# Theta from float16 parts of x that DMA turns, v kept from its sizing, and a new order of the steps: a planned attention and mixing kernel on one core

## The chip, the cores and the metric

The kernel runs on one core of one Trainium2 chip. The metric is the device time of one execution in microseconds; several runs are made and their median is taken. The engines are TensorE (PE; its weight loads are shown apart as PEld), VectorE (DVE), ScalarE (ACT), GpSimd (POOL) and SyncE (SP), which issues the DMA transfers.

## The reference

```python
def _attn_ref(q, k, v):                      # 8 batches, 8 heads, 576 rows, 64 columns
    scores = scale * np.matmul(q, k.transpose(0, 1, 3, 2))
    scores = np.where(block_i >= block_j, scores, -1000000000.0)   # blocks of 64 rows
    attn = np.exp(scores - np.max(scores, axis=-1, keepdims=True))
    attn = attn / (np.sum(attn, axis=-1, keepdims=True) + 1e-09)
    return np.matmul(attn, v)

def _moe_ref(x, w_theta, w_tok_r, w_tok_i, w_ch):   # x: 8 x 576 x 512, the heads side by side
    theta = x @ w_theta
    zr, zi = x * np.cos(theta), x * np.sin(theta)
    u = x + np.einsum('ts,bsd->btd', w_tok_r, zr) + np.einsum('ts,bsd->btd', w_tok_i, zi)
    return u + np.maximum(u @ w_ch, 0.0)
```

q, k, v are float32, the weights float64 (read as two words each). Theta is large, so its product has to be accurate.

## The kernel before, in words

Every product is made in parts: an operand is rounded to a short type (the high part) and what is left is rounded again (the low part); high x high, low x high and high x low are added in PSUM. q, k, theta's x, u, w_theta and w_ch have float32r parts, p (the exponentials), v, z and w_tok float16 parts.

Two heads are a pair, four pairs a batch. Per pair q and k are loaded, rounded on GpSimd (L471, L475), and their low parts made on VectorE for q (L479) and on GpSimd for k (L484). TensorE makes the scores (L506, L520, the mask L514), VectorE the row maxima (L533), ScalarE the exponentials (L537) and their high part (L546), VectorE their low part (L549). A DMA transposition (L553, `pt<-p`, 24 or 26 blocks of 128x128 for one head) turns them, and TensorE multiplies them by v (L565, L570); VectorE divides by the row sums into `xn` (L577, L579, L585).

v is scaled by a power of two per batch so that its float16 parts hold. For that all four pairs' v are loaded into `vz` (L436), ScalarE sums their sizes (L439), GpSimd spreads the sums on a diagonal (L324), TensorE brings them together (L328) and VectorE makes the power (L335 to L344). Later each v is loaded once more, into `v` (L488), for its parts (L491, L494). x comes out scaled in the same way.

Per batch the mixer follows. TensorE transposes x, 20 blocks (L623); ScalarE rounds it out of PSUM and removes the scale (`xh`, L634), VectorE makes the low part (`xl`, L638). Theta (L647) is 5 groups of 12 matmuls of 512 columns. Its turns and remainders come from L655 and L660, sizes, cosines and sines from ScalarE (L666 to L674), the products with x from GpSimd (L682), their parts z from L691 and L696. The mixing over tokens (L706) is 8 groups of 27 matmuls of 288 columns; VectorE adds the high part of x to it (L711), GpSimd the low part (L716). u's parts are made by ScalarE (L719) and GpSimd (L723), the channel product (L731) is 8 groups of 12 matmuls, VectorE finishes (L737) and the result is stored (L741).

The weights are prepared while batch 0 runs. Each float64 row block is loaded as words (L370). ScalarE scales the high word, read as a float32, by 2^-112 (L379), VectorE shifts it (L386), puts the sign back (L388) and adds the low word's bits (L391). w_tok is sized as v is, over all its blocks (L395, L413 to L423), and its parts are made on ScalarE (L399) and VectorE (L405); those of w_theta and w_ch on ScalarE (L401) and GpSimd (L408).

What runs when is a list. Every step is added under a key with the steps that it needs; `TIMES` holds one number per step, the steps are issued in the order of these numbers, each engine takes its own in that order, and `BANKS` names the PSUM bank that each step takes. The numbers only sort:

```python
    order = sorted(zip(TIMES, range(len(TIMES)), parts), key=lambda x: x[:2])
```

A tile used again needs the steps that read it last (`turn_of`).

Of the kernel before, what the change touches and what calls it, by code (L numbers as in the profile page):

```python
# [27 lines left out]
QK_BUFS = 2  # L28
# [5 lines left out]
    845, 1285, 1406, 1509, 1716, 1838, 1919, 315, 755, 830, 880, 1012, 1094, 1175, 1150, 2754, 3004, 3252, 3631,  # L34
    3713, 4155, 1430, 2267, 3150, 3318, 3563, 3645, 3869, 1825, 2610, 3699, 3803, 3995, 4128, 9220, 9303, 2105,
    2550, 3114, 3186, 3735, 3817, 9286, 9383, 3875, 4394, 4521, 4629, 4960, 5042, 9020, 9223, 3695, 4334, 4557,
    5405, 5539, 5670, 8781, 9703, 4235, 4675, 5276, 5339, 5471, 5821, 8715, 9017, 4055, 4495, 4593, 5607, 6229,
    6311, 9484, 9623, 5095, 5610, 7069, 7181, 7315, 7403, 9418, 9543, 6245, 6710, 6903, 6995, 7113, 7269, 8847,
    8937, 5615, 6055, 6297, 6400, 7247, 7336, 9352, 9463, 7205, 7645, 7863, 8223, 8375, 8457, 8538, 7510, 7950,
    8113, 8289, 8690, 8913, 9097, 7790, 8230, 11402, 11530, 11734, 11981, 12305, 8635, 9696, 9783, 9932, 10224,  # L40
    10548, 10767, 7627, 7809, 8111, 8355, 8535, 8607, 8633, 8682, 0, 345, 495, 840, 1025, 1370, 1610, 1986, 2085,
    2113, 2164, 2205, 2239, 2261, 2283, 2475, 2285, 2670, 3570, 3915, 4415, 4760, 5400, 5888, 6015, 6057, 6268,
    6476, 6939, 6987, 7061, 7105, 6425, 6770, 7080, 7470, 8510, 9116, 9245, 9612, 9819, 9887, 9938, 10130, 10216,
    10292, 10489, 11331, 9945, 10325, 10424, 10854, 11089, 11517, 11859, 12231, 12495, 12519, 12650, 12738, 12865,
    12927, 13096, 13118, 12444, 13954, 14053, 14434, 14533, 14878, 15088, 15486, 15596, 15730, 18326, 18393, 18427,
# [900 lines left out]
```

## Time and profile before

| | |
|---|---|
| median of 3 runs | 780.52 us (779.15 to 782.35) |
| the profiled execution | 782.25 us, its span 780.3 us |
| mean granted TensorE clock | 0.969 |
| share of the span: PE, PEld, DVE, ACT, POOL | 89%, 75%, 71%, 64%, 52% |
| read from HBM, written | 54.59 MB, 9.44 MB |
| moved by DMA | 117.66 MB, of 232420 packets 209680 under 512 B |

Busy PE time counts matmuls that overlap, with ends that are modelled; so lengths of long runs of matmuls in the chain of waits are the better price of TensorE's work. A group in the table of groups is one line, engine, operation and shape; its last column is the idle time of the engine just before and what ended it.

### The profile page before, as it was taken

How to read it: one execution, taken by the hardware profiler on the slowest of the kernel's cores; microseconds unless marked ns; L12 is line 12 of the kernel's file. 1: busy time of each engine (PE TensorE's matmuls, PEld its weight loads, DVE VectorE, ACT ScalarE, POOL GpSimd, SP SyncE). 2: the span in 40 equal slices, each digit the busy share in tenths (PEclk: the TensorE clock that was granted, in tenths of full speed). 3: DMA queues.
4: the chain of work that ended last, by engine and by line, in shares of the span. 5: the costliest groups of instructions: out<-in, count | busy, mean ns of one | idle time of the engine just before them, and what ended most of it. 6: DMA issues, size and time to landing. Idle time of an engine off the chain costs nothing.

```text
span 780.3 us, 18483 instructions
## 1 busy us (share of the span) xinstructions
PE 695.9 (89%) x7657; PEld 588.8 (75%) x7657; DVE 551.4 (71%) x995; ACT 499.4 (64%) x780; POOL 408.5 (52%) x413
## 2 busy tenths in 40 slices
PE   3536479788999999999999999999999999999987
PEld 2435368676897878887898788878898889778866
DVE  5799998669757895688955987397847985543221
ACT  4778788866885776756793577466774678335220
POOL 3331332883348660886348552974178613850860
PEclk9986779999999999999999999999999999999999
DMA  8989997688838995469735785596736962430101
GB/s 286 226 266 273 235 216 202 163 167 206 198 95 205 200 198 120 95 134 193 166 132 105 156 157 136 117 176 146 155 102 120 201 140 65 78 76 1 61 1 61
DMA packets 232420, 117.66 MB, mean 151 GB/s; under 512 B 209680, under 2 KB 209680, under 8 KB 232336
## 3 DMA queue, kind: packets, MB, share of 16 engines
q1 hardware_dynamic: 232336, 116.48, 64.4%
q8 instruction: 60, 0.98, 0.5%
q14 instruction: 24, 0.20, 0.1%
HBM read 54.59 MB, written 9.44 MB: 82 GB/s over the span
## 4 chain that ended last, share of the span: by engine, by line
PE 61%; DMA 12%; DVE 12%; POOL 5%; issue 5%; ACT 4%; POOLq 0%; ACTq 0%; SPq 0%; DVEq 0%
PE ps L706 18%; PE ps L647 14%; PE ps L731 13%; DMA pt<-p 10%; PE ps L506 7%; PE ps L565 6%; DVE m L533 3%; DVE p L549 2%; DMA vz<-in_v 2%; DVE v L494 1%; POOL u L716 1%; ACT t L537 1%; ACT p L546 1%; POOL ul L723 1%; POOL zl L696 1%
## 5 line engine op out<-in xcount | busy, mean ns | idle before, releaser
L537 ACT ACTIVATE t<-ps,m 128x576 f32<-128x576 f32 (+4 forms) x288 | 143.5, 553 | 74.0 <-DVE m L533 55.8
L706 PE MATMUL ps<-wT_h,zh 128*128 128x288 f16 x576 | 166.7, 289 | 5.3 <-ACT t L537 4.3
L706 PE MATMUL ps<-wT_h,zl 128*128 128x288 f16 x576 | 166.2, 289 | 2.4 <-POOL zl L696 1.8
L706 PE MATMUL ps<-wT_l,zh 128*128 128x288 f16 x576 | 166.3, 289 | 0.0
L533 DVE TENSOR_REDUCE m<-ps 128x1 f32<-128x192 f32 (+4 forms) x288 | 133.6, 510 | 19.2 <-PE ps L514 17.3
L549 DVE SCALAR_TENSOR_TENSOR p<-t,p 128x1536 f16<-128x1536 f32 (+1 forms) x64 | 124.3, 1944 | 31.9 <-ACT p L546 31.8
L706 PEld LDWEIGHTS <-zh 128*128 128x128 f16 x1152 | 113.5, 99 | 31.1 <-ACT zh L691 1.1
L565 PE MATMUL ps<-v,pt 128*128 128x65 f16 x2688 | 98.5, 198 | 30.1 <-DVE xn L585 22.3
L565 PEld LDWEIGHTS <-pt 128*128 128x128 f16 x2688 | 93.5, 101 | 36.1 <-DMA pt<-p 18.2
L546 ACT ACTIVATE p<-t 128x1536 f16<-128x1536 f32 (+1 forms) x64 | 96.6, 1516 | 36.3 <-DMA pt<-p 35.9
L682 POOL TENSOR_TENSOR aa<-aa,xn 128x256 f32<-128x256 f32 (+1 forms) x96 | 70.2, 758 | 75.6 <-PE ps L731 27.9
L506 PE MATMUL ps<-kh,qh 64*128 64x64 f32 (+4 forms) x384 | 73.0, 360 | 20.2 <-ACT t L537 10.9
L731 PE MATMUL ps<-uh,wch_h 128*128 128x288 f32 x256 | 78.3, 306 | 1.8 <-ACT uh L719 1.6
L731 PE MATMUL ps<-ul,wch_h 128*128 128x288 f32 x256 | 76.3, 298 | 1.1 <-POOL ul L723 1.1
L731 PE MATMUL ps<-uh,wch_l 128*128 128x288 f32 x256 | 76.3, 298 | 0.0
L706 PEld LDWEIGHTS <-zl 128*128 128x128 f16 x576 | 56.9, 99 | 22.1 <-POOL zl L696 5.2
L723 POOL TENSOR_TENSOR ul<-u,uh 128x576 fp32r<-128x576 f32 x32 | 56.4, 1769 | 23.8 <-ACT uh L719 23.8
L716 POOL TENSOR_TENSOR u<-u,xl 128x576 f32<-128x576 f32 x32 | 47.5, 1490 | 39.6 <-DVE u L711 30.3
L737 DVE SCALAR_TENSOR_TENSOR u<-ps,u 128x288 f32<-128x288 f32 x64 | 29.1, 455 | 55.3 <-PE ps L731 54.2
L506 PEld LDWEIGHTS ps<-kh,qh 64*128 64x128 f32 x384 | 41.6, 201 | 33.1 <-ACT t L537 13.2
L647 PE MATMUL ps<-wth_h,xh 128*128 128x512 f32 x160 | 65.3, 408 | 1.3 <-DVE xl L638 1.3
L506 PE MATMUL ps<-kh,ql 64*128 64x64 f32 (+4 forms) x384 | 64.9, 327 | 0.0
(98 smaller groups left out, 1490.9 us busy)
## 6 DMA issues: line engine op xcount, KB each, us to landing
vz<-in_v SPq DMA_DIRECT2D x32, 384.0 KB, 3.9
v<-in_v SPq DMA_DIRECT2D x32, 384.0 KB, 3.8
q<-in_qT SPq DMA_DIRECT2D x32, 320.0 KB, 3.5
k<-in_kT SPq DMA_DIRECT2D x32, 288.0 KB, 3.7
out<-u SPq DMA_DIRECT2D x32, 288.0 KB, 2.1
w_raw<-in_w_tok SPq DMA_DIRECT2D x9, 576.0 KB, 4.4
w_raw<-in_w_theta SPq DMA_DIRECT2D x4, 512.0 KB, 6.2
w_raw<-in_w_ch SPq DMA_DIRECT2D x4, 512.0 KB, 5.0
```

Of the source, the lines that this page charges most:

```text
L506: nc.tensor.matmul(s[hh][:, col:col + n], lhsT=qq[rows, i * P:(i + 1) * P], rhs=kk[rows, k0:k0 + n], start=nn == 0 and col % BANK == 0, st ...
L533: nc.vector.tensor_reduce(out=m, in_=s, axis=AX.X, op=ALU.max, negate=True)
L537: nc.scalar.activation(out=to, in_=s, func=AF.Exp, scale=1.0, bias=m)
L546: nc.scalar.mul(self.p[:, 0, 0:self.width], self.t, LIFT)
L549: nc.vector.scalar_tensor_tensor(out=self.p[:, 1, 0:self.width], in0=self.t, scalar=LIFT, in1=self.p[:, 0, 0:self.width], op0=ALU.mult, op ...
L565: nc.tensor.matmul(o[:, i, :], lhsT=pp[:, block, :], rhs=vv[:, of, hh, :], start=nn == 0, stop=nn == n - 1)
L647: nc.tensor.matmul(g, lhsT=xx[:, dt, i * P:(i + 1) * P], rhs=ww[:, dt, :], start=(n == 0), stop=(n == 11))
L682: nc.gpsimd.tensor_tensor(out=cd, in0=cd, in1=self.rows(dt, i0, ni), op=ALU.mult)
L706: nc.tensor.matmul(g, lhsT=zz[:, kk, cols], rhs=ww[:, kk, ts], start=(n == 0 and kk == k0 and nn == 0), stop=(n == 4 and nn == 2))
L716: nc.gpsimd.tensor_tensor(out=u, in0=u, in1=self.x_parts()[1].bitcast(F32)[:, dt, 0:S], op=ALU.add)
L723: nc.gpsimd.tensor_tensor(out=ul[:, dt, :], in0=self.u(dt), in1=uh[:, dt, :].bitcast(F32), op=ALU.subtract)
L731: nc.tensor.matmul(g[:, 0:HS], lhsT=ww[:, dt, e * P:(e + 1) * P], rhs=uu[:, dt, th * HS:(th + 1) * HS], start=(n == 0), stop=(n == 11))
```

## The change

- **Theta in float16.** x stays in the scale of v. It is rounded into float16 parts of one tile `xt` (two of them, taken in turn by the batches), w_theta is sized as w_tok is and gets float16 parts (its low part now on VectorE), and the scales of x and w_theta are taken out where theta becomes turns (`turn`).
- **DMA turns x.** In batches 1 to 7 the parts are made from `xn` in SBUF, on ScalarE and VectorE (`xp`, 128x640), and four DMA transpositions of 10 blocks bring them into `xt`. Batch 0 keeps TensorE's transposition.
- **v kept from its sizing.** v is loaded once, into a tile per pair of the batch (`raw_v`); sizing and parts both read it.
- **Exponents by a slope.** ScalarE's scaling of the high word uses a slope of -2^32 for negative values, so that VectorE's step that put back the sign (old L388) is gone.
- **Two steps on VectorE.** k's low part moves there from GpSimd. x's sum is made there ahead of time, high + low into u (L728), then unscaled (L731); the mixing is added to that, and GpSimd's sum (old L716) is gone.
- **A new order.** TIMES and BANKS are new. In the new order theta of one batch stands inside the mixing of the batch before it.

The core of the diff (line numbers of the changed kernel are those used for it below):

```diff
 TIMES = [
-    845, 1285, 1406, 1509, 1716, 1838, 1919, 315, 755, 830, 880, 1012, 1094, 1175, 1150, 2754, 3004, 3252, 3631,
...
@@
-    wth_h = const.tile([P, NDT, DM], F32R, name="wth_h")
+    wth_h = const.tile([P, NDT, DM], F16, name="wth_h")
...
+    raw_v = const.tile([P, NPAIR, NV * P], F32, name="raw_v")
...
-            nc.scalar.mul(self.val, self.high.bitcast(F32), 2.0 ** -112)
+            nc.scalar.activation(out=self.val, in_=self.high.bitcast(F32), func=AF.Prelu, scale=2.0 ** -112, alpha=-2.0 ** 32)
...
-            elif step == 1:
-                nc.vector.scalar_tensor_tensor(out=bits, in0=self.high, scalar=0x80000000, in1=bits,
-                                               op0=ALU.bitwise_and, op1=ALU.bitwise_or)
...
+        def sum_of(self, pr):
+            n = (NV - 1) * P
+            nc.scalar.activation(out=unused, in_=raw_v[:, pr, 0:n], func=AF.Abs, accum_out=self.sums[:, pr:pr + 1])
...
+                nc.gpsimd.tensor_scalar(out=self.turn, in0=self.down, scalar1=w_down["theta"], scalar2=TURN,
+                                        op0=ALU.mult, op1=ALU.mult)
...
-            nc.gpsimd.tensor_tensor(out=self.kl, in0=self.k, in1=self.kh.bitcast(F32), op=ALU.subtract)
+            nc.vector.tensor_tensor(out=self.kl, in0=self.k, in1=self.kh.bitcast(F32), op=ALU.subtract)
...
         def x_parts(self):
-            return [self.tile_of(tag, [P, NDT, 640], F32R) for tag in ("xh", "xl")]
+            return self.tile_of(f"xt{self.b % 2}", [P, NDT, 2, NI, P], F16)
...
+        def x_pieces(self, dt):
+            if self.b:
+                if dt not in self.xp:
+                    self.xp[dt] = at.tile([P, 2, NI, P], F16, tag="xp", name="xp")
+                return [self.rows(dt, 0, NI).rearrange("p i h d -> p i (h d)")] + [self.xp[dt][:, part] for part in range(2)]
...
         def x_high(self, dt):
-            for g, xh, _ in self.transposed(dt):
-                nc.scalar.mul(xh, g, self.batch.down)
+            x, high, _ = self.x_pieces(dt)
+            nc.scalar.copy(out=high, in_=x)
...
+            nc.vector.tensor_tensor(out=low, in0=x, in1=high, op=ALU.subtract)
+
+        def x_turn(self, dt):
+            nc.sync.dma_start_transpose(out=self.x_parts()[:, dt].rearrange("p a i q -> p (a i) q"),
+                                        in_=self.xp[dt].rearrange("p a i c -> p (a i c)"))
...
-                for xx, ww in ((xh, wth_h), (xl, wth_h), (xh, wth_l)):
-                    nc.tensor.matmul(g, lhsT=xx[:, dt, i * P:(i + 1) * P], rhs=ww[:, dt, :], start=(n == 0), stop=(n == 11))
+                for part, ww in ((0, wth_h), (1, wth_h), (0, wth_l)):
+                    nc.tensor.matmul(g, lhsT=x[:, dt, part, i, :], rhs=ww[:, dt, :], start=(n == 0), stop=(n == 11))
...
+        def add_parts(self, dt):
+            high, low = (self.x_parts()[:, dt, part].rearrange("p i q -> p (i q)")[:, 0:S] for part in range(2))
+            nc.vector.tensor_tensor(out=self.u(dt), in0=high, in1=low, op=ALU.add)
+
+        def unscale(self, dt):
+            nc.vector.tensor_scalar(out=self.u(dt), in0=self.u(dt), scalar1=self.batch.down, scalar2=None, op0=ALU.mult)
...
         def take_u(self, dt, th):
...
-                                           in1=self.x_parts()[0].bitcast(F32)[:, dt, ts], op0=ALU.mult, op1=ALU.add)
-
-        def add_low(self, dt):
-            u = self.u(dt)
-            nc.gpsimd.tensor_tensor(out=u, in0=u, in1=self.x_parts()[1].bitcast(F32)[:, dt, 0:S], op=ALU.add)
+                                           in1=self.u(dt)[:, ts], op0=ALU.mult, op1=ALU.add)
...
-            add(("vq", b, pr), step_of(batch.load, pr), turn_of("vz", [("vs", b, pr)]))
-            add(("vs", b, pr), step_of(batch.sum, pr), [("vq", b, pr)])
...
+            add(("v", p), pairs[p].load_v, turn_of(f"raw_v{pr}", [("v2", p)]))
+            add(("vz", p), step_of(batch.sum_of, pr), [("v", p)])
...
+            for dt in range(NDT):
+                part("xh", (dt,), m.x_high, [("normalise", 8 * b + 2 * dt + hh, 2) for hh in range(2)] + turn_of("xp", [("xt", b, dt)]))
+                part("xl", (dt,), m.x_low, [("xh", b, dt)])
+                part("xt", (dt,), m.x_turn, [("xl", b, dt)] + x_free)
```

Two places of the order. The first is TensorE's row near the end of the program, where the last head of batch 7 has been multiplied by v; the names are `pt` the turned exponentials, `xn` the normalised x, `wth` and `wT` the parts of w_theta and w_tok. Before (L570 the attention product, L623 x's transposition, L647 theta):

```order
L570 LDWEIGHTS pt_101
L570 MATMUL ps<-v_85,pt_101 64x65
L623 MATMUL ps<-ident_r,xn 128x128 x20
L647 MATMUL ps<-wth_h,xh 128x512
L647 MATMUL ps<-wth_h,xl 128x512
```

After (L583 the attention product, L723 the mixing of batch 6):

```order
L583 LDWEIGHTS pt_101
L583 MATMUL ps<-v_85,pt_101 64x65
L723 LDWEIGHTS zh
L723 MATMUL ps<-wT_h,zh 128x288
L723 LDWEIGHTS zl
L723 MATMUL ps<-wT_h,zl 128x288
```

The 20 transpositions are gone from the row, and 57 matmuls of the mixing of batch 6 now stand between the last head and theta of batch 7; before, all of that mixing stood ahead of the last head.

The second is VectorE's row in the middle of the program. Before, the low parts of x (L638) are taken out of PSUM between row maxima (L533), row sums (L577, L579) and the low part of p (L549):

```order
L533 TENSOR_REDUCE m<-ps 128x1 x4
L638 SCALAR_TENSOR_TENSOR xl<-ps,sizes,xh 128x512
L638 SCALAR_TENSOR_TENSOR xl<-ps,sizes,xh 128x4x128
L577 TENSOR_SCALAR r<-ps 128x4
L549 SCALAR_TENSOR_TENSOR p_97<-t_95,p_97 128x1536
L579 RECIPROCAL r<-r 128x4
```

After, x's sums (L728) and their unscaling (L731) stand among the row maxima (L546), the normalisation (L598) and z's low part (L713); L598 is followed further on by x's low part out of SBUF (L652), and k's low part is a VectorE step (L498):

```order
L728 TENSOR_TENSOR u_4250<-xt_3057 128x576
L728 TENSOR_TENSOR u_4274<-xt_3057 128x576
L731 TENSOR_SCALAR u_4250<-u_4250,sizes 128x576
L546 TENSOR_REDUCE m<-ps 128x1 x3
L598 TENSOR_TENSOR xn<-ps,r 128x4x64
L546 TENSOR_REDUCE m<-ps 128x1
L713 TENSOR_TENSOR zl<-aa,zh 128x256
L731 TENSOR_SCALAR u_4274<-u_4274,sizes 128x576
```

VectorE's row gains per batch 4 sums, 4 unscalings and 4 low parts of k, and has 4 low parts of x of 640 columns where 5 of 512 stood.

More of the change, by code (lines that the diff above doesn't have):

```diff
@@ L410, in attention_phase_mixer, with w_reduce, w_diagonal, w_all @@
     w_g = {}
-    def w_reduce():
-        nc.vector.tensor_reduce(out=w_size[:, 4:5], in_=w_most, axis=AX.X, op=ALU.max)
-    def w_diagonal():
-        w_g["diag"] = mo.tile([P, P], BF16, tag="zl", name="w_diag")
-        diagonal(w_g["diag"], w_size[:, 4:5])
-    def w_all():
-        all_sizes(bank("w"), w_g["diag"])
-    def w_scale(step):
-        power_of_two(bank("w") if step < 0 else None, w_size, step, 151.0)
-    sizes = const.tile([P, B, 10], F32, name="sizes")
+    def w_reduce(kind):
+        nc.vector.tensor_reduce(out=w_size[kind][:, 4:5], in_=w_most[kind], axis=AX.X, op=ALU.max)
+    def w_diagonal(kind):
+        w_g[kind] = mo.tile([P, 1, P], BF16, tag={"theta": "zh", "tok": "zl"}[kind], name="w_diag")
+        diagonals(w_g[kind], w_size[kind][:, 4:5])
+    def w_all(kind):
+        all_sizes(bank("w", kind), w_g[kind])
+    def w_scale(kind, step):
+        parts = (w_size[kind][:, i:i + 1] for i in range(4))
+        power_of_two(bank("w", kind) if step < 0 else None, *parts, step, 151.0)
+    sizes = const.tile([P, B, 11], F32, name="sizes")
+    unused = const.tile([P, (NV - 1) * P], BF16, name="unused")
     class Batch:
@@ L790, in attention_phase_mixer @@
         for step in range(-1, 4):
-            add(("vc", b, step), step_of(batch.scale, step), [("vc", b, step - 1) if step >= 0 else ("vm", b)],
+            add(("vc", b, step), step_of(batch.powers, step), [("vc", b, step - 1) if step >= 0 else ("vm", b)],
                 leaves=() if step >= 0 else [("v", b)])
+        for i, kind in enumerate(("tok", "theta")):
+            add(("us", b, i), step_of(batch.unit_of, i), [("vc", b, 3), ("wc", kind, 3)])
     mixers = [Mixer(b, batches[b]) for b in range(B)]
@@ L835, in attention_phase_mixer @@
                 if step == 2 and hh == 0:
-                    needs = needs + turn_of("xn", [("g", b, pr), ("g", b, NDT)] + [("z", b, pr // 2, i) for i in range(5)],
+                    needs = needs + turn_of("xn", ([("xl", b, pr)] if b else [("g", b, pr), ("g", b, NDT)]) + [("z", b, pr // 2, i) for i in range(5)],
                                             X_BUFS)
@@ L859, in attention_phase_mixer @@
         for i in range(NI):
-            needs = w_last["theta"] + [("xl", b, dt) for dt in (range(NDT) if i < 4 else [NDT])]
+            needs = w_last["theta"] + [key for dt in range(NDT) for key in (x_done[dt] if b else [("xl", b, dt if i < 4 else NDT)])]
             part("theta", (i,), m.theta, needs + free, takes=[("t", 1)])
-            part("turns", (i,), m.turns, [("theta", b, i)])
+            part("turns", (i,), m.turns, [("theta", b, i), ("us", b, 1)])
             part("rest", (i,), m.rest, [("turns", b, i)], leaves=[("t", 1)])
```

157 lines of the change are left out of this document (81 added, 76 removed), and 370 rows, old and new, of tables (BANKS, TIMES).

## The prediction

> **What bounds the kernel now.** I read the page's busy times first, then the busy times by stage, then the chain of waits.
>
> ```profile
> PE 695.9 (89%) x7657; PEld 588.8 (75%) x7657; DVE 551.4 (71%) x995; ACT 499.4 (64%) x780; POOL 408.5 (52%) x413
> ```
>
> The share alone would say "TensorE, with 11% to spare". Cut by stage it says something else (columns: length, then the busy microseconds of PE, PEld, DVE, ACT, POOL, the granted clock, the DMA share, GB/s):
>
> ```profile
> 0.00:40.00 40.00, 17.84 (x114) 14.14 (x114) 26.14 (x46) 23.92 (x41) 14.60 (x34) 1.00 0.94 259
> 40.00:140.00 100.00, 62.70 (x766) 53.82 (x766) 94.17 (x178) 80.67 (x137) 32.59 (x31) 0.81 0.91 234
> 140.00:740.00 600.00, 583.23 (x6560) 494.12 (x6561) 421.81 (x756) 389.74 (x595) 346.33 (x339) 1.00 0.63 138
> 740.00:780.00 40.00, 32.11 (x219) 26.75 (x217) 9.31 (x17) 5.07 (x9) 15.01 (x11) 0.91 0.08 30
> ```
>
> There are two regimes. From 40 to 140 us VectorE is busy 94 of 100 us and TensorE runs at a granted clock of 0.81: the preparation of the weights on VectorE, with transfers at a share of 0.91 to 0.94, sets the pace. From 140 to 740 us TensorE is busy 583.2 of 600 us; 16.8 us of idle is all that better waiting could give there. The chain agrees:
>
> ```profile
> PE 61%; DMA 12%; DVE 12%; POOL 5%; issue 5%; ACT 4%; POOLq 0%; ACTq 0%; SPq 0%; DVEq 0%
> ```
>
> So work taken off TensorE after 140 us shortens the time, and work put on VectorE costs only as far as it makes TensorE wait. These pieces of the chain, in order of time (start, length), price the TensorE work:
>
> ```profile
> 202.68 14.05 PE ps L647 x60
> 290.35 14.25 PE ps L647 x60
> 377.17 1.31 PE ps L623 x12
> 701.43 14.30 PE ps L647 x60
> 728.56 13.26 PE ps L706 x108
> ```
>
> The theta product L647 of batch 1 starts at 202.68 and that of batch 7 at 701.43: six batches, 83.1 us each. One theta matmul (float32r, 512 columns) takes 14.25/60 = 237.5 ns; one of the mixing (float16, 288 columns, L706) 13.26/108 = 122.8 ns; one transposition of x (L623) 1.31/12 = 109 ns.
>
> **The change part by part.** *Theta in float16.* The number of matmuls stays at 480. By columns, a float16 matmul of 512 costs 512/288 x 122.8 = 218.3 ns, which saves 19.2 ns each. The 420 of batches 1 to 7 (60 each) lie in the TensorE regime: 8.1 us. Bounds: nothing, if 512 columns cost the same in both types, and 10 us (an estimate), if part of the 122.8 ns is fixed per matmul and does not grow with the columns. I take 8.1. The 60 of batch 0 lie where VectorE sets the pace; I count nothing.
>
> *Transpositions off TensorE.* 20 in each of batches 1 to 7: 140 x 109 ns = 15.3 us, all in the TensorE regime. In their place stand four DMA transpositions of 10 blocks per batch, each behind the last step of x on VectorE. What they cost goes by the rows of the 24- and 26-block turns (the chain, then the transfers with their median time to landing):
>
> ```profile
> 533.76 7.37 DMA pt<-p
> ```
> ```profile
> vz<-in_v SPq DMA_DIRECT2D x32, 384.0 KB, 3.9
> v<-in_v SPq DMA_DIRECT2D x32, 384.0 KB, 3.8
> pt<-p SPq DMA_TRANSPOSE x64, 6.4
> ```
>
> 10 of 25 blocks of 7.37 us are 2.9 us. Per batch 11.8 us of transposing come and four loads of v (vz) go, 15.6 us by their time to landing; the DMA share of 0.63 does not rise by much. For theta the path from x lengthens by two or three microseconds, and the order shows what TensorE does in that time: at the end of the last batch, the first place shown in the section on the change, the 20 transpositions are gone, and 57 mixing matmuls (57 x 122.8 ns = 7.0 us) moved in ahead of theta; in the other batches the matmuls between the two are worth 9 to 21 us by the same rows. They hide the turn; without that cover it would cost its 2.9 us and a wait on VectorE, some 5 us, per batch.
>
> The Trainium skill's page "VectorE: DVE Perf Modes", section "The three transpose paths", speaks against this edit: it gives a DMA transposition 1309 ns per 128x128 block against 390 ns on TensorE. By it 10 blocks would be 13 us (an estimate), 6 us more than the last batch's cover, and 25 blocks 33 us. The trace does not agree: 24 or 26 blocks took 7.37 us in the row above, and the sum goes by that.
>
> *VectorE.* These groups (line, engine, operation, tiles, shapes, count, busy us, mean ns, idle before) price it:
>
> ```profile
> L388 DVE SCALAR_TENSOR_TENSOR w_val<-w_raw,w_val 128x576 uint32<-128x576 uint32 x9 | 7.7, 864 | 0.0
> L388 DVE SCALAR_TENSOR_TENSOR w_val<-w_raw,w_val 128x512 uint32<-128x512 uint32 x8 | 6.4, 822 | 0.0
> L386 DVE TENSOR_SCALAR w_val<-w_val 128x576 uint32<-128x576 uint32 x9 | 4.4, 507 | 0.0
> L405 DVE SCALAR_TENSOR_TENSOR wT_l<-w_val,w_size,wT_h 128x576 f16<-128x576 f32 x9 | 7.7, 924 | 0.0
> L638 DVE SCALAR_TENSOR_TENSOR xl<-ps,sizes,xh 128x512 fp32r<-128x512 f32 x40 | 28.4, 740 | 4.9 <-ACT xh L634 3.1 <-POOL ul L723 1.7
> L484 POOL TENSOR_TENSOR kl<-k,kh 128x576 fp32r<-128x576 f32 x32 | 49.9, 1559 | 1.4
> L716 POOL TENSOR_TENSOR u<-u,xl 128x576 f32<-128x576 f32 x32 | 47.5, 1490 | 39.6 <-DVE u L711 30.3 <-DVE r L579 4.4 <-ACT zh L691 2.3
> L479 DVE SCALAR_TENSOR_TENSOR ql<-q,qh 128x640 fp32r<-128x640 f32 x32 | 33.4, 1044 | 6.8 <-POOL qh L471 6.7
> ```
> ```profile
> 200.00:700.00 500.00, 491.27 (x5643) 418.11 (x5643) 364.15 (x652) 327.90 (x495) 286.56 (x273) 1.00 0.65 142
> ```
>
> In a batch of the middle VectorE is busy 364.15/500 x 83.1 = 60.5 us. By ql's 1044 ns for 640 elements, 576 cost 940 ns. Added per batch: k's low part 4 x 0.94 = 3.8 us, x's sum 4 x 0.94 = 3.8, its unscaling 4 x 0.51 = 2.0, x's low part 4 x 1.04 in place of 5 x 0.74 = 0.5. That is 10.1 us: 70.6 us, in a batch that TensorE now needs for 83.1 - 1.15 - 2.2 = 79.8 us. VectorE goes from 73% to 88%, GpSimd loses 4 x (1.56 + 1.49) = 12.2 us of 47.6.
>
> In VectorE's row of the middle (the second place shown) the new sums stand ahead of row maxima (L546) and of x's normalisation (L598), so softmax and the next scores queue behind them on VectorE, and TensorE behind those. How often that reaches TensorE I read from two 20 us windows in which VectorE was already that full:
>
> ```profile
> 180.00:200.00 20.00, 17.94 (x236) 14.52 (x236) 18.61 (x39) 14.21 (x26) 9.32 (x8) 1.00 0.85 192
> 360.00:380.00 20.00, 19.72 (x261) 16.85 (x260) 19.33 (x36) 15.45 (x25) 12.32 (x9) 1.00 0.80 170
> ```
>
> TensorE idled 2.1 and 0.3 us in them. Bounds for what the middle gives back: nothing, by the second, and at the top idle that grows as VectorE's room shrinks: 22.6 us of room per batch become 9.2, a factor of 2.5, so 16.8 x 1.5 = 25 us. The second window speaks for the lower half; I take 10.
>
> *A port that VectorE and GpSimd share.* All three new kinds of step read SBUF twice; the old xl read PSUM. The timeline shows what that can cost (start, length):
>
> ```profile
> 5.62 0.83 DVE L479 SCALAR_TENSOR_TENSOR ql<-q,qh 128x640 fp32r<-128x640 f32 x1 [3.50 <-POOL qh L471]
> 11.65 1.88 DVE L479 SCALAR_TENSOR_TENSOR ql<-q,qh 128x640 fp32r<-128x640 f32 x1 [1.45 <-POOL qh L471]
> 11.58 1.27 POOL L408 TENSOR_TENSOR wth_l<-w_val,wth_h 128x512 fp32r<-128x512 f32 x1
> ```
>
> The same ql took 0.83 us alone and 1.88 us when a GpSimd step was under way: 1.05 us, about what was left of that step (1.20). ql's mean of 1.04 is therefore 0.2 us of blocking, and it is in my prices. The Trainium skill's page "SBUF — State Buffer", section "Who interferes with whom", states this as a lock: a VectorE instruction with two SBUF inputs and a GpSimd one that reads SBUF exclude each other whole. The two rows agree with it. It is the mechanism of rival B.
>
> *The start.* Each v is loaded once and its sum of sizes runs over 640 elements instead of 768, on ScalarE, off the path. Ahead of the first remainder of batch 0 (the first step after theta) the order has 16 sign steps L388 fewer, 7 x 0.822 + 9 x 0.864 = 13.5 us, and more: 6 low parts of k (0.75 each, by the undisturbed ql: 4.5), 4 low parts of theta (512/576 x 0.924: 3.3), theta's sizing (some 1 us, an estimate from its six small steps), 2 sums (1.9). VectorE nets 2.8 us less. Loads: the first in line was v for sizing, and the chain starts with it:
>
> ```profile
> 0.75 3.12 DMA vz<-in_v
> ```
>
> Now k and q go first; I count those 3.1 us. Up to the eighth turn of p there are 8 loads of v instead of 17. Together -5.9 us; bounds 0 and -15 (the nine loads at 259 GB/s are 14 us, if transfers set the pace). The slope on ScalarE replaces a multiplication of the same size, with 16 table loads in both orders: nothing.
>
> *The end.* Between the last mixing and the last channel product one GpSimd sum leaves the path:
>
> ```profile
> 759.53 1.41 POOL u L716
> ```
>
> -1.4 us; what is late next is the rounding of u, which follows at once.
>
> **Sum.** -8.1 - 15.3 - 5.9 - 1.4 + 10 = -20.7 us. The profiled execution took 782.25 us (span 780.3), 1.7 above the median of the three runs, 780.52. So 761.6 against its own time, 760 as a median. By the bounds: -10 - 15.3 - 15 - 1.4 + 0 = 739 at best; 0 - 15.3 + 0 - 1.4 + 25 = 789 at worst.
>
> **The rivals.** *A, VectorE takes it all back.* The give-back of 25 us meets the gain of 30.7: 780.52 - 5.7 = 775, and with a start that gains nothing 781, no change. For: 88% with in-order queues. Against: the window at 360 us, VectorE at 97% and TensorE at 98.6%.
>
> *B, slower: the port lock makes VectorE the bound.* Twelve new two-input steps per batch. If each met a GpSimd step as the ql at 11.65 did (1.88 instead of 0.83), they cost 12 x 0.84 us over my prices (which hold 0.2 of the 1.05), 10 us more: 70.6 + 10.1 = 80.7 us per batch. Where VectorE sets the pace today, from 40 to 140 us, it is busy 94.17 of 100, so a batch would last 80.7/0.942 = 85.7 us, 2.6 more than now: 780.5 + 7 x 2.6 - 5.9 - 1.4 = 791. It makes the kernel slower by over 0.5% from a batch of 84.7 us on, that is from 0.77 us over my price per step. Against: GpSimd sheds 12.2 us per batch, so there is less to meet.
>
> *C, the turned x comes late.* If in each of seven batches theta waited the 5 us in spite of its cover: 760 + 35 = 795 at most; if in two, 770. For: SP's queue gets 28 turns and loses 32 loads; each turn waits there for x's low part on VectorE, with loads of q, k and v and turns of p queued behind it, and itself stands behind stores that wait for the channel product. Against: 7 to 21 us of cover. I weigh the case of two.
>
> *D, the start gains its bound.* 760 - 9 = 751. For: transfers at 0.94. Against: VectorE's 94% stays.
>
> **How the numbers follow.** Forecast 0.62, A 0.10 (half of it no change), B 0.08, C 0.10 (a third of it not faster), D 0.10. Half a per cent, 3.9 us, is about what a measurement here can tell from no change. Faster: 0.62 + 0.05 + 0.07 + 0.10 = 0.84; no change: 0.05 + 0.02 = 0.07; slower: 0.08 + 0.01 = 0.09. The range holds D, the forecast with half its give-back either way, C in two batches and the faster half of A: 747 to 776.
>
> **What would show it.** Right: theta's 60 in about 13.1 us; no L623 after batch 0; a theta-to-theta period near 81 us; VectorE's new steps at 0.75 to 1.1 us; PE idle of the middle under 30 us; theta of batch 0 some 6 us earlier. Wrong: float16 theta at 237 ns; PE waiting for the DMA turn of x at its first matmul; new VectorE steps at 1.5 us and more; VectorE over 95% in the middle with TensorE under 93%.

## The result, and the profile after

The changed kernel takes 757.17 us (median of 4 runs, 755.6 to 760.83) against 780.74 us for the kernel before (4 runs): a ratio of 0.9705 [0.9664, 0.9746] (in brackets the 95% interval). A second measurement of the same kernel, beside the experiments, gave 0.9735 [0.9708, 0.9762]. The forecast was 760 us, faster; both lie inside its range.

The profiled execution took 756.52 us, its span 754.6 us. Line numbers are now those of the changed kernel (theta L664, mixing L723, channel product L751, x's parts L648 and L652, its turn L655, x's sum L728, its unscaling L731). First the busy times, the chain's shares and the bytes of the page:

```profile
PE 674.8 (89%) x7518; PEld 532.4 (71%) x7518; DVE 599.9 (79%) x1077; ACT 497.1 (66%) x781; POOL 331.5 (44%) x354
PE 47%; DVE 25%; DMA 11%; ACT 11%; issue 5%; POOL 1%; POOLq 0%; SPq 0%; ACTq 0%; DVEq 0%
HBM read 42.01 MB, written 9.44 MB: 68 GB/s over the span
```

TensorE's share is the same 89% of a shorter span. What changed is the chain: TensorE holds 47% of it instead of 61%, VectorE 25% instead of 12%, ScalarE 11% instead of 4%, and GpSimd's 5% are down to 1%. v's second loads are gone from the bytes read (54.59 MB before).

The busy times by stage (length, then PE, PEld, DVE, ACT, POOL, the granted clock, the DMA share, GB/s; the last row lies inside the one above it):

```profile
0.00:40.00 40.00, 20.36 (x135) 15.47 (x136) 30.47 (x63) 29.66 (x60) 9.19 (x30) 1.00 0.92 282
40.00:140.00 100.00, 68.82 (x848) 52.70 (x846) 91.97 (x173) 82.85 (x133) 26.97 (x30) 0.81 0.83 190
140.00:714.00 574.00, 551.70 (x6287) 435.50 (x6284) 466.56 (x824) 379.10 (x580) 280.94 (x282) 0.99 0.68 144
200.00:674.00 474.00, 455.26 (x5370) 363.80 (x5369) 399.44 (x712) 323.29 (x493) 232.12 (x233) 0.99 0.71 150
```

From 140 us on TensorE idles 574 - 551.7 = 22.3 us (16.8 before), and VectorE is busy 399.4/474 = 84% of the middle (73% before, 88% forecast). From 40 to 140 us VectorE is still the fullest engine, at 92 of 100 us, with more of TensorE's work beside it (68.8 us instead of 62.7).

Pieces of the chain that price TensorE's work now (start, length):

```profile
185.74 12.95 PE ps L664 x60
269.73 13.07 PE ps L664 x60
410.07 5.93 DMA xt<-xp
672.17 7.09 PE ps L723 x57
679.26 5.18 PE ps L664 x24
```

A theta matmul takes 12.95/60 = 215.8 ns (217.8 by the second row; 237.5 before). The 57 mixing matmuls stand ahead of the last theta, as the order showed, and take 7.09 us.

**Where the time went.** I use two marks, the first theta matmul of batch 0 and that of batch 7. Batch 7's is at 701.43 before and 679.26 after, in the chains. Batch 0's is the first start in the rows of theta's line in each trace (count, duration min/median/max in ns, first and last start); before:

```profile
L647 PE MATMUL ps<-wth_h,xh x160: 392/397/632, 115.4 to 714.9; 128*128 128x512 f32 x160
```

and after:

```profile
L664 PE MATMUL ps<-wth_h,xt x320: 376/379/634, 102.6 to 692.7; 128*128 128x512 f16 x160
```

The start gained 115.4 - 102.6 = 12.8 us, the stretch between the marks 586.03 - 576.66 = 9.37 us, and the rest 78.87 - 75.34 = 3.53 us: 25.7 us of span. One caution: nine mixing matmuls of batch 6 (1.1 us) now stand behind the second mark. On equal work the middle gained 8.3 us and the end 4.6. The forecast had 5.9, 12.2 (15.3 and 6.9, less 10) and 2.6.

How far the marks of one trace can be trusted shows in the other traces of this document. The stretch between the marks, by first starts, is steady: 576.5 and 575.9 us in the two traces of the changed kernel, 586.0 and 586.1 in two of the kernel before (the second with one load moved). The first mark is not: in the traces whose edit leaves the start as it is, it stands between 102.6 and 108.4 us. So 12.8 us is the upper end of what the start gained; the two measured differences, 23.6 and 20.3 us, less 9.4 for the middle and 3.5 for the end, leave 10.7 and 7.4.

**The start.** These are VectorE's costliest changed groups ahead of the first mark, before (busy us, mean ns):

```profile
L388 DVE SCALAR_TENSOR_TENSOR w_val<-w_raw,w_val 128x576 uint32<-128x576 uint32 (+1 forms) x16 | 13.4, 854 | 0.0
L391 DVE SCALAR_TENSOR_TENSOR w_val<-w_raw,w_val 128x576 uint32<-128x576 uint32 (+1 forms) x16 | 12.8, 812 | 0.0
L405 DVE SCALAR_TENSOR_TENSOR wT_l<-w_val,w_size,wT_h 128x576 f16<-128x576 f32 x9 | 7.7, 924 | 0.0
L479 DVE SCALAR_TENSOR_TENSOR ql<-q,qh 128x640 fp32r<-128x640 f32 x7 | 6.8, 971 | 5.8 <-POOL qh L471 5.8
L494 DVE SCALAR_TENSOR_TENSOR v<-v,sizes,v 128x768 f16<-128x768 f32 x4 | 5.2, 1298 | 0.0
```

and after:

```profile
L391 DVE SCALAR_TENSOR_TENSOR w_val<-w_raw,w_val 128x576 uint32<-128x576 uint32 (+1 forms) x16 | 11.8, 752 | 0.0
L406 DVE SCALAR_TENSOR_TENSOR wT_l<-w_val,size_tok,wT_h 128x576 f16<-128x576 f32 x9 | 7.0, 806 | 0.0
L493 DVE SCALAR_TENSOR_TENSOR ql<-q,qh 128x640 fp32r<-128x640 f32 x8 | 6.8, 845 | 1.5 <-POOL qh L485 1.5
L498 DVE TENSOR_TENSOR kl<-k,kh 128x576 fp32r<-128x576 f32 x6 | 4.5, 754 | 4.0 <-POOL kh L489 4.0
L507 DVE SCALAR_TENSOR_TENSOR v<-raw_v,sizes,v 128x768 f16<-128x768 f32 x4 | 4.1, 1014 | 0.0
L406 DVE SCALAR_TENSOR_TENSOR wth_l<-w_val,size_theta,wth_h 128x512 f16<-128x512 f32 x4 | 3.0, 746 | 0.2 <-ACT wth_h L400 0.2
```

The sign step's 13.4 us went, 4.5 and 3.0 us came. But steps that the change does not touch are shorter too: adding the low word 812 to 752 ns, w_tok's low part 924 to 806, q's 971 to 845, v's 1298 to 1014; by their counts some 4 us together. The windows up to the mark say the same; before and after, in that order:

```profile
0.00:115.40 115.40, 57.98 (x679) 49.41 (x679) 99.00 (x186) 83.09 (x146) 38.67 (x55) 0.85 0.96 252
```
```profile
0.00:102.60 102.60, 57.48 (x678) 48.22 (x679) 89.47 (x179) 79.71 (x144) 21.56 (x44) 0.86 0.93 244
```

VectorE did 9.5 us less work and idled 3.3 us less (16.4 to 13.1), which is the 12.8 us. GpSimd's work ahead of the mark fell from 38.7 to 21.6 us. That the untouched steps got shorter because of it is borne out in part by the run below that gives k's low part back to GpSimd: there, ahead of the mark, q's low part takes 1063 ns and v's 1290 again, though w_tok's stays at 806.

### The profile page after: what moved, and what is told of

Its sections match the earlier page's. It is cut to its first block, busy times and chain, and to the rows that moved or that the text cites. A ratio compares the mean times of both kernels' runs of the same rounds, so it can differ in the third digit from the quotient of the medians.

```text
span 754.6 us, 18218 instructions
## 1 busy us (share of the span) xinstructions
PE 674.8 (89%) x7518; PEld 532.4 (71%) x7518; DVE 599.9 (79%) x1077; ACT 497.1 (66%) x781; POOL 331.5 (44%) x354
## 4 chain that ended last, share of the span: by engine, by line
PE 47%; DVE 25%; DMA 11%; ACT 11%; issue 5%; POOL 1%; POOLq 0%; SPq 0%; ACTq 0%; DVEq 0%
PE ps L723 14%; PE ps L664 10%; PE ps L751 10%; DMA pt<-p 7%; PE ps L519 7%; DVE p L562 6%; PE ps L578 5%; DVE m L546 5%; ACT t L550 3%; DMA raw_v<-in_v 2%; DVE u L731 2%; ACT p L559 2%; DVE u L728 2%; DVE v L507 2%; DVE kl L498 1%
## 5 line engine op out<-in xcount | busy, mean ns | idle before, releaser
L550 ACT ACTIVATE t<-ps,m 128x320 f32<-128x320 f32 (+4 forms) x288 | 142.8, 554 | 45.9 <-DVE m L546 23.4
L723 PE MATMUL ps<-wT_h,zh 128*128 128x288 f16 x576 | 167.0, 290 | 6.2 <-ACT t L550 3.8
L723 PE MATMUL ps<-wT_h,zl 128*128 128x288 f16 x576 | 166.4, 289 | 3.7 <-DVE zl L713 2.8
L723 PE MATMUL ps<-wT_l,zh 128*128 128x288 f16 x576 | 166.2, 289 | 0.0
L546 DVE TENSOR_REDUCE m<-ps 128x1 f32<-128x448 f32 (+4 forms) x288 | 133.6, 512 | 16.3 <-PE ps L527 13.8
L723 PEld LDWEIGHTS <-zh 128*128 128x128 f16 x1152 | 113.6, 99 | 33.7 <-ACT zh L708 1.9
L562 DVE SCALAR_TENSOR_TENSOR p<-t,p 128x1536 f16<-128x1536 f32 (+1 forms) x64 | 121.0, 1895 | 16.8 <-ACT p L559 16.4
L699 POOL TENSOR_TENSOR aa<-aa,xn 128x256 f32<-128x256 f32 (+1 forms) x96 | 88.2, 946 | 24.8 <-ACT aa L689 24.8
L519 PE MATMUL ps<-kh,qh 64*128 64x64 f32 (+4 forms) x384 | 77.9, 365 | 21.8 <-ACT t L550 13.6
L664 PE MATMUL ps<-wth_h,xt 128*128 128x512 f16 x320 | 95.9, 382 | 0.7 <-DVE rr L677 0.6
L664 PEld LDWEIGHTS <-xt 128*128 128x128 f16 x480 | 46.7, 99 | 54.7 <-issue 2.1
L743 POOL TENSOR_TENSOR ul<-u,uh 128x576 fp32r<-128x576 f32 x32 | 50.7, 1589 | 76.0 <-ACT uh L739 75.9
L751 PE MATMUL ps<-uh,wch_h 128*128 128x288 f32 x256 | 79.3, 310 | 2.2 <-ACT t L550 0.8
L699 POOL TENSOR_TENSOR rr<-rr,xn 128x256 f32<-128x256 f32 x64 | 59.7, 956 | 45.7 <-ACT rr L691 45.7
L751 PE MATMUL ps<-ul,wch_h 128*128 128x288 f32 x256 | 75.6, 295 | 0.6 <-POOL ul L743 0.6
L751 PE MATMUL ps<-uh,wch_l 128*128 128x288 f32 x256 | 75.4, 294 | 0.0
L723 PEld LDWEIGHTS <-zl 128*128 128x128 f16 x576 | 56.9, 99 | 24.6 <-DVE zl L713 3.8
L519 PEld LDWEIGHTS ps<-kh,qh 64*128 64x128 f32 x384 | 45.5, 206 | 36.9 <-ACT t L550 15.4
L489 POOL TENSOR_SCALAR kh<-k 128x576 fp32r<-128x576 f32 x32 | 27.3, 852 | 99.4 <-DMA k<-in_kT 37.4
```

The lines of the kernel that those rows point to most:

```text
L489: nc.gpsimd.tensor_scalar(out=self.kh, in0=self.k, scalar1=1.0, scalar2=0.0, op0=ALU.mult, op1=ALU.add)
L519: nc.tensor.matmul(s[hh][:, col:col + n], lhsT=qq[rows, i * P:(i + 1) * P], rhs=kk[rows, k0:k0 + n], start=nn == 0 and col % BANK == 0, st ...
L546: nc.vector.tensor_reduce(out=m, in_=s, axis=AX.X, op=ALU.max, negate=True)
L550: nc.scalar.activation(out=to, in_=s, func=AF.Exp, scale=1.0, bias=m)
L562: nc.vector.scalar_tensor_tensor(out=self.p[:, 1, 0:self.width], in0=self.t, scalar=LIFT, in1=self.p[:, 0, 0:self.width], op0=ALU.mult, op ...
L664: nc.tensor.matmul(g, lhsT=x[:, dt, part, i, :], rhs=ww[:, dt, :], start=(n == 0), stop=(n == 11))
```

## The experiments

Twelve kernels ran, each timed in five rounds beside the kernel before on the same chip. The theory: the stages have different limits, so TensorE's work pays after 140 us, VectorE's before it, and VectorE gives a part back in the middle. The rivals: VectorE alone sets the pace everywhere; the port lock with GpSimd is the cost; the transfers do it.

**The changed kernel again**, unedited, as the base for the others.

> The changed kernel again, unedited, on the chip of the next three: 757 us (755 to 761), a ratio to the kernel before of 0.970. Every theory expects the same; it is the base for the others.

758.96 us, 0.9735 [0.9708, 0.9762].

**The transpositions back on TensorE.** In batches 1 to 7 theta's bank first gets four transpositions of the identity per group, 20 per batch, overwritten by theta. No other engine has a part in them.

```diff
+            if self.b:
+                for j in range(4):
+                    nc.tensor.transpose(out=g[:, j * P:(j + 1) * P], in_=ident, identity=ident)
```

> Puts TensorE's transposing back in batches 1 to 7: four transpositions of the identity ahead of each theta group, into the bank that the group then overwrites; 140 in all, of 109 ns, and nothing waits for them. Theory 1 (after 140 us TensorE still sets the pace, so its work is on the path): +15.3 us, 772. Theory 2 (VectorE, busy 84% in the middle, sets the pace now, so TensorE has room): at most +5, 757 to 762.

770.77 us, 0.9883 [0.985, 0.9916]: 11.8 us more than the changed kernel, give or take some 3 by the two intervals. 140 x 109 ns are 15.3 us, so about 77% of TensorE's time reaches the end, between the two theories and nearer to the first. TensorE sets the pace in most of the middle; whether in all of it, this run alone hardly tells.

**No sum of x.** x's sum (L728) and unscaling (L731) are left out; the mixing adds x's high part as it is.

```diff
-            nc.vector.tensor_tensor(out=self.u(dt), in0=high, in1=low, op=ALU.add)
+            pass
-            nc.vector.tensor_scalar(out=self.u(dt), in0=self.u(dt), scalar1=self.batch.down, scalar2=None, op0=ALU.mult)
+            pass
```

> Leaves out x's sum and its unscaling on VectorE: the mixing is added to x's high part as it stands, so x's low part and its scale are missing from u. VectorE loses 30.4 + 24.5 = 55 us of 600. Theory 1: TensorE's stalls shrink a little, -2 to -6 us, 751 to 755. Theory 2: VectorE sets the pace in the middle, 48 us less there: -12 us or more, under 745.

747.63 us, 0.9593 [0.956, 0.9625]: 11.3 us less. In the changed kernel these steps are 30.4 + 24.5 = 54.9 us of VectorE, so about 21% of VectorE's time reaches the end (15 to 27% by the intervals). That lies between the two theories: VectorE counts for more than small stalls, and does not set the pace alone.

**Both at once**: the transpositions on TensorE and no sum.

> Both at once: x's sum and unscaling left out on VectorE (x's low part and scale missing from u) and TensorE's 140 transpositions put back. Alone they gave -11.3 and +11.8 us to the changed kernel's 759. Theory 1 (TensorE sets the pace and VectorE's queue makes holes in it; the holes are what swallowed part of the transpositions): without VectorE's work the transpositions cost their whole 15.3, 763. Theory 2 (each engine sets the pace in places of its own, and the two add up): 759 to 760.

760.44 us, 0.9747 [0.9719, 0.9774]. Without the sum the same transpositions cost 0.0154 of 781 us, 12.0 us, as much as with it, which favours theory 2. But theory 1 does not fall: its 763 us lie at the upper edge of the interval (759 to 763). The traces do not settle it either. Of the 140 transpositions, 124 lie between the marks, 13.5 us. With the sum in the kernel they lengthen that stretch from 575.9 to 587.2 us, by 11.3; without it from 566.3 to 580.9, by 14.6. Yet the granted clock of these four stretches is 0.98, 0.99, 0.99 and 0.98, in that order, and a hundredth of such a stretch is nearly 6 us. Whether VectorE's steps hide part of TensorE's price stays open.

**k's low part back on GpSimd.**

```diff
-            nc.vector.tensor_tensor(out=self.kl, in0=self.k, in1=self.kh.bitcast(F32), op=ALU.subtract)
+            nc.gpsimd.tensor_tensor(out=self.kl, in0=self.k, in1=self.kh.bitcast(F32), op=ALU.subtract)
```

> k's low part back on GpSimd, at the same place in the order. VectorE loses 30.4 us, GpSimd gains 45 to 50 us and is busy 50% instead of 44%. Theory 1: off the path either way, within 3 us of 757. Theory 2 (VectorE is the bound): -6 us or more, 751. Theory 3 (the shared port: each GpSimd step of 1.4 us holds VectorE up longer than the 0.95 us that it takes on VectorE): +3 to +8, 760 to 765.

757.57 us, 0.9719 [0.9679, 0.976]: no difference that can be measured. Why it gained nothing stands in VectorE's groups. With k's low part on VectorE (the unedited kernel):

```profile
L507 DVE SCALAR_TENSOR_TENSOR v<-raw_v,sizes,v 128x768 f16<-128x768 f32 x32 | 35.3, 1102 | 0.6 <-ACT v L504 0.6
L493 DVE SCALAR_TENSOR_TENSOR ql<-q,qh 128x640 fp32r<-128x640 f32 x32 | 29.2, 911 | 1.0 <-POOL qh L485 1.0
L498 DVE TENSOR_TENSOR kl<-k,kh 128x576 fp32r<-128x576 f32 x32 | 28.8, 899 | 4.3 <-POOL kh L489 4.3
L652 DVE TENSOR_TENSOR xp<-xn,xp 128x640 f16<-128x640 f32 x28 | 27.2, 972 | 3.2 <-ACT xp L648 3.2
```

and with it on GpSimd:

```profile
L507 DVE SCALAR_TENSOR_TENSOR v<-raw_v,sizes,v 128x768 f16<-128x768 f32 x32 | 41.9, 1309 | 1.0 <-ACT v L504 0.9
L493 DVE SCALAR_TENSOR_TENSOR ql<-q,qh 128x640 fp32r<-128x640 f32 x32 | 35.3, 1103 | 8.0 <-POOL qh L485 8.0
L652 DVE TENSOR_TENSOR xp<-xn,xp 128x640 f16<-128x640 f32 x28 | 32.3, 1154 | 2.5 <-ACT xp L648 2.5
```

The windows from 140 to 640 us, with it on VectorE and then with it on GpSimd:

```profile
140.00:640.00 500.00, 483.13 (x5552) 380.29 (x5550) 422.19 (x744) 348.53 (x538) 245.01 (x249) 0.98 0.73 152
```
```profile
140.00:640.00 500.00, 478.59 (x5555) 378.02 (x5553) 421.87 (x721) 348.54 (x539) 292.65 (x273) 0.99 0.73 153
```

28.8 us of steps left VectorE over the whole kernel, and its busy time is the same, 599.4 us with them and 599.6 without (in the window 422, with 23 steps fewer): v's low parts took 6.6 us longer over the whole kernel, q's 6.1, x's 5.1, p's longer form 3.1, and others a little each. GpSimd is 47.6 us busier in the window; the steps that grew read SBUF twice, as those that the forecast saw held up by a GpSimd step.

**x's sum on GpSimd**, the unscaling still on VectorE.

```diff
-            nc.vector.tensor_tensor(out=self.u(dt), in0=high, in1=low, op=ALU.add)
+            nc.gpsimd.tensor_tensor(out=self.u(dt), in0=high, in1=low, op=ALU.add)
```

> x's sum (32 steps, 30.4 us on VectorE) moves to GpSimd at the same place in the order, where two SBUF inputs of 576 took 1.4 us alone before: 45 to 50 us. Theory 1 (VectorE's time counts): 30.4/55 of 11.3, -6 us, 753. Theory 2 (as with k's low part, which moved to GpSimd gave -1.4 us: GpSimd's longer step holds the shared port and takes the gain back): within 3 us of 759. Theory 3 (the sum in GpSimd's queue holds up the products with x): slower, 763.

760.1 us, 0.972 [0.9686, 0.9754]: no difference again. Here VectorE's busy time does fall, from 599.4 to 588.3 us, though by far less than the 30.4 us that left it. In these two trials a step with two SBUF inputs cost the kernel the same on either of the two engines.

**The unscaling on ScalarE.**

```diff
-            nc.vector.tensor_scalar(out=self.u(dt), in0=self.u(dt), scalar1=self.batch.down, scalar2=None, op0=ALU.mult)
+            nc.scalar.mul(self.u(dt), self.u(dt), self.batch.down)
```

> x's unscaling (32 steps, 24.5 us, mean 776 ns, 420 to 510 where GpSimd is idle) moves from VectorE to ScalarE at the same place in the order; ScalarE gains some 21 us. Leaving out both sum and unscaling gave 11.3 us for 55 us of VectorE. Theory 1 (what counts is VectorE's time, whatever the step): 24.5/55 of it, -5 us, 754. Theory 2 (the sum is what TensorE's work waits behind, the unscaling has room): within 2 us of 759. Theory 3 (ScalarE's queue, 66% busy, is as sensitive): +2 to +5.

754.21 us, 0.9662 [0.9633, 0.9692]: the fastest version with all of the work in it, 3.4 us (by the first measurement of the changed kernel, whose interval it overlaps) to 5.7 us (by the second, whose interval it does not) less. That is up to half of what the sum and the unscaling cost together.

**That, and k's low part on GpSimd** (the edits of both).

> x's unscaling on ScalarE (alone -5 us) and k's low part on GpSimd (alone -1 us). Theory 1 (VectorE's time counts, GpSimd's does not): -6 us or more against the changed kernel, 752 to 753. Theory 2 (a longer GpSimd step takes back through the shared port what VectorE sheds): no better than the unscaling alone, 754 to 756.

756.03 us, 0.9686 [0.9658, 0.9714]: no better than the unscaling alone, as theory 2 had it. Room made on VectorE does not change the verdict on k's low part.

**The sign step back** on VectorE, behind ScalarE's slope.

```diff
+                nc.vector.scalar_tensor_tensor(out=bits, in0=self.high, scalar=0x80000000, in1=bits,
+                                               op0=ALU.bitwise_and, op1=ALU.bitwise_or)
```

> Puts the sign step back on VectorE, once per weight block ahead of the low word's bits (17 steps of 0.68 to 0.75 us, some 12 us, 16 of them ahead of the first step after theta of batch 0); the bits it sets are there already. Theory 1 (the start gained because VectorE had less to do there): +8 to +12, 767 to 771. Theory 2 (the start gained because v is loaded once and k and q come first): under +3, 762 at most.

765.86 us, 0.981 [0.9776, 0.9844]: 6 to 8 us more, by the two measurements of the changed kernel: at or below the lower end of theory 1, clearly above theory 2. Up to its first theta matmul:

```profile
0.00:113.80 113.80, 60.67 (x679) 51.05 (x680) 100.86 (x194) 80.23 (x144) 22.42 (x44) 0.88 0.83 218
```

VectorE is busy 100.9 us instead of 89.5 (90.1 in the repeat), and theta comes at 113.8, later than in any trace with the unedited start (102.6 to 108.4). The stretch behind the mark is as long as without the step (574.8 us). So VectorE's work counts in the start: of the 11.4 us put back there, 5 to 11 show at the mark, and half to three quarters at the end.

**v loaded twice.** Each load is followed by one more, into a tile that nothing reads.

```diff
+            vz = ld.tile([P, NV, 2, D], F32, tag="vz", name="vz")
+            nc.sync.dma_start(out=vz, in_=v[self.b, self.pr])
```

> Loads each v a second time into a tile that nobody reads, right behind the first load in SP's queue: 32 transfers of 384 KB, 12.6 MB, as many as before the change. Theory 1 (VectorE set the pace of the start): under +3, 762 at most. Theory 2 (transfers did): 8 of these loads, 3.1 MB at 280 GB/s, fall in the first 100 us, +6 to +11, 765 to 770.

762.08 us, 0.9767 [0.9734, 0.98]: 2.5 to 5 us more, at the edge of what is told apart. In its trace the first mark stands at 104.9 us (104.8 in the unedited kernel of the experiments), so the start does not pay for these loads. The stretch between the marks is 579.9 us, 3.4 to 4.0 more than in the two unedited traces, at a granted clock of 0.97 instead of 0.98. So what the loads cost, if anything, falls in the middle.

**The kernel before, with q and k first.** One number of TIMES moves the first load of v behind the first loads of q and k.

```diff
-    10548, 10767, 7627, 7809, 8111, 8355, 8535, 8607, 8633, 8682, 0, 345, 495, 840, 1025, 1370, 1610, 1986, 2085,
+    10548, 10767, 7627, 7809, 8111, 8355, 8535, 8607, 8633, 8682, 240, 345, 495, 840, 1025, 1370, 1610, 1986, 2085,
```

> The kernel before with one number of its order changed: the first load of v for sizing is issued behind the first q and k instead of ahead of them. The chain began with 3.12 us of that load. Theory 1 (it holds up the first scores, and they the start): -2 to -3 us, 777. Theory 2 (VectorE is behind by then and the start does not care): within 1 us of 780.

782.1 us, 1.0023 [1.0004, 1.0042]: nothing is gained. But the edit did not take the load off the chain. In this run's trace the chain still goes through it, now from 1.68 us on, behind the issues of q and k, and 5.26 us long. So the run shows that loading q and k ahead of it gains nothing; it does not show what the start is worth without that load. The changed kernel's own chain does that better. It begins with a load of nearly the same length:

```profile
0.75 2.89 DMA k<-in_kT
```

**x turned twice.** A second DMA turn of each x into a tile that nothing reads.

```diff
+            again = ld.tile([P, 2, NI, P], F16, tag="again", name="again")
+            nc.sync.dma_start_transpose(out=again.rearrange("p a i q -> p (a i) q"),
+                                        in_=self.xp[dt].rearrange("p a i c -> p (a i c)"))
```

> Turns x's parts a second time by DMA into a tile that nobody reads: 28 more turns of 10 blocks right behind the first ones in SP's queue. Theory 1 (the turn lies beside other work): under +2, 761 at most. Theory 2 (transfers in the middle delay the turns of p, as v's second load did with +3 us, all of it after the start): +3 to +6, 762 to 765.

769.24 us, 0.9849 [0.9822, 0.9876]: 9 us more, above both theories, though nothing waits for the result. Its waits (total, times, longest) and its transfers (count, median us to landing):

```profile
PEld L578 <- DMA pt<-p: 15.7, 13, 3.1
PE ps L578 <- DMA pt<-p: 12.9, 10, 3.0
ACT xp L648 <- DMA again<-xp: 11.6, 4, 3.8
```
```profile
pt<-p SPq DMA_TRANSPOSE x64, 7.1
```

and the same in the unedited kernel:

```profile
PEld L578 <- DMA pt<-p: 9.4, 8, 3.3
PE ps L578 <- DMA pt<-p: 3.9, 4, 1.6
ACT xp L648 <- DMA xt<-xp: 2.1, 2, 1.6
```
```profile
pt<-p SPq DMA_TRANSPOSE x64, 6.3
```

Two things happen. The turns of p land later (7.1 us instead of 6.3, medians) and the product with v waits for them, 9.0 us more on TensorE. And x's next rounding on ScalarE waits until the turn has read `xp`, of which there is one, with exponentials queued behind it. The run doesn't tell how the 9 us split between the two, nor what part comes from SP's queue alone: issuing a turn of x takes 1.4 to 1.8 us there (rows of the changed kernel at 410.07 and 418.29), a load of k or v 0.53.

## Why the prediction was right, point by point

- **What bounds the kernel: right in the main.** TensorE's work after 140 us and VectorE's work before it both reached the end for the most part, by experiment.
- **Theta in float16: right.** 215.8 ns per matmul, 218.3 forecast; 420 x 21.7 ns = 9.1 us of TensorE's time instead of 8.1. How much of it reaches the end was not tried alone.
- **Transpositions off TensorE: right, a size perhaps off.** 11.8 and 12.0 us, each give or take some 3, where the sum had 15.3. It priced every TensorE microsecond of the middle in full, with 16.8 us of idle there in plain sight.
- **DMA turns of x counted at nothing: half right.** Theta never waits for them; its only wait in the trace is 0.6 us for a remainder on VectorE. Rival C as it was put, with theta waiting, did not come: the cover held. But the step looked only at the consumer. It did not look at who waits to refill `xp` (ScalarE, 3.0 us in three waits here), nor at p's turns, which share the transfers. One turn stands on the chain, at 410.07, and releases just that rounding. What the first turn costs is open: between little and the 9 us of the second. The 1309 ns per block of the Trainium skill's page "VectorE: DVE Perf Modes", section "The three transpose paths", are not what these turns show: the 10 blocks of x land in 4.0 us (median).
- **VectorE gives back 10: right in size, wrong in kind.** The sum and the unscaling alone cost 11.3 us, give or take some 3. k's low part, which the forecast priced at 3.8 us of VectorE per batch beside them, costs nothing that can be measured, since VectorE's other steps get shorter by as much. x's new steps came out as priced (k's 951 ns and the sum's 959 for 940, x's low part 992 for 1040), but the unscaling took 776 ns for 510. Rows of the timeline show why (start, length): one at 107.71 with no GpSimd step beside it, and one at 395.35 that begins inside a GpSimd step:

```profile
107.71 0.51 DVE L731 TENSOR_SCALAR u<-u,sizes 128x576 f32<-128x576 f32 x1
...
394.85 1.60 POOL L713 TENSOR_TENSOR zl<-rr,zh 128x512 f16<-128x512 f32 x1
395.35 1.41 DVE L731 TENSOR_SCALAR u<-u,sizes 128x576 f32<-128x576 f32 x1
396.41 0.93 POOL L485 TENSOR_SCALAR qh<-q 128x640 fp32r<-128x640 f32 x1
```

  The GpSimd step had 1.10 us left when the second began; 0.51 and most of that make its 1.41. So the unscaling was held up as the forecast saw a step with two inputs from SBUF held up. (Its undisturbed ql, 0.83 us at 5.62, was not alone throughout: a GpSimd step began beside it at 6.03 and did not lengthen it. What counted there is which step came first.) The forecast had the lock for steps with two inputs from SBUF only. The Trainium skill's page "SBUF — State Buffer", section "Who interferes with whom", names it for one-input steps of this kind as well, in a mode that takes both ports; these rows agree with it.
- **Rival B, the lock makes VectorE the bound: its mechanism is there, its end is not.** VectorE came to 84% of the middle, not above the 88% of the sum. GpSimd had less left to block it with (331.5 us busy instead of 408.5), as the argument against the rival said; that this is the reason was not tried.
- **The start, -5.9: too small.** It was 12.8 us in the two profiles and 7 to 11 by the medians. The step that failed is "VectorE nets 2.8 us less": it was 9.5. The two sums (1.9 us) run behind the first theta matmul, which is the mark here (the first begins at 103.3), and steps that the change does not touch became some 4 us shorter, with 17 us less of GpSimd's work ahead of the mark. The term of 3.1 us for the first load was worth next to nothing: a load of k, 2.89 us long, now begins the chain in its place. v's second loads were worth nothing in the start either; if they paid, it was in the middle, where the sum had nothing for them.
- **The end, -1.4 and theta's 1.2:** 4.6 us on equal work. Theta's 60 matmuls gave 1.3. The GpSimd sum gave 0.4, not 1.4: between the last mixing and the last channel product lie 4.69 us before and 4.33 after, since the low part of u, 1.41 us on GpSimd, now stands on the chain there. Most of the rest is a lower clock in the kernel before, which no one had forecast. Its last two long runs of matmuls, and the same two after:

```profile
743.88 14.60 PE ps L706 x104
763.17 13.62 PE ps L731 x89
```
```profile
723.11 11.82 PE ps L723 x95
739.26 11.68 PE ps L751 x86
```

  A mixing matmul took 140.4 ns before and 124.4 after, a channel matmul 153.0 and 135.8: together 3.2 us for the 193 of them. The granted clock in these four stretches was 0.88 and 0.87 before, 1.00 and 1.00 after. The last channel product was slow in both traces of the kernel before (13.62 and 14.77 us) and in none of the twelve of the changed kernel and its variants (11.68 to 11.69); why the clock differs there is open.
- **The middle as a sum.** Transpositions -12, theta's 360 matmuls -7.8 by their pitch, v's loads -3, sum and unscaling +11.3: -11.5, against 8.3 measured between the marks on equal work. The 3.2 us left are what the first turn and the new order may have cost, or the clock, granted at 0.99 between the marks before and at 0.98 after. Three of the terms are known to some 3 us each, so this remainder is no measurement. The theta-to-theta period, which the forecast named as a sign, came down from 83.1 to (679.26 - 185.74)/6 = 82.3 us, not to 81.
- **The good fit of 760 to 757 is in part luck.** A middle forecast 4 us too large met a start forecast 1.5 to 5 us too small and an end 2 us too small, most of that end being the clock.

## What to carry to other kernels

Ask of each microsecond on which engine and in which stage it lies, and what part of it reaches the end: here about three quarters of TensorE's in the middle, a fifth of VectorE's there, and half to three quarters of VectorE's in the start. Where VectorE and GpSimd hold each other up, shifting a step between the two may move nothing, as in both trials here; try a third engine (the unscaling on ScalarE gave the best version, 754.21 us). Put the granted clock beside every stretch that is compared: part of what the end gained here was a clock, not the edit. A transfer that nobody waits for still has a price: look at who refills its source, and at the transfers behind it.

## What the runs showed of the hardware that was not expected

- Taking 28.8 us of steps off VectorE and giving them to GpSimd left VectorE's busy time where it was (599.4 and 599.6 us): a busy engine may be waiting inside its instructions.
- A step with one input from SBUF, 576 float32 columns by a scalar, took 0.51 us without a GpSimd step and 1.41 beside one.
- 28 more DMA turns of 10 blocks lengthened the median landing of p's 64 turns from 6.3 to 7.1 us.
- In the last stretch of the kernel before, a channel matmul took 153.0 ns at a granted clock of 0.87, in that of the changed kernel 135.8 ns at 1.00.
